# The router logits of a finished item move from between two steps into the next step's first layer

## The chip, the cores and the metric

One core of one Trainium2 chip runs the whole program as one launch. The metric is the device time of that launch in microseconds, as the median of several runs. Before the change it is 465.76 us.

## What is computed

Attention over blocks (8 heads, 576 positions, 2 batches) gives 1152 rows of 512 numbers. Two mixtures of experts follow, each with 8 experts of two layers (512 to 1024 to 512), and each row goes to one expert:

```python
x = _moe_ref(x=x, **moe_kwargs)
return _moe2_ref(x=x, **moe2_kwargs)
...
logits = x @ w_gate
e_idx = np.argmax(logits, axis=1)
...
h = np.maximum(x[mask] @ w1[e], 0.0)
ye = h @ w2[e]
out[mask] = gate_w[mask, None] * eom[mask, e, None] * ye
```

The second mixture needs `logits = x @ w_gate` of the first one's output, for all rows, before it can pick the expert of each row. It also keeps the rows in their order, since an expert takes no more than a given number of them.

## The kernel before

The rows of one mixture are grouped by expert into **items** of up to 128 rows. In this data the first mixture has 10 items (0 to 9), which the program learns at run time. One **step** handles one item: `layer1` (L1254, products at L602), a relu on ScalarE (L1261), 8 transposes on TensorE (`htrans`, L1267), and `layer2` (L1286, products at L616). The inputs are 32-bit floats, and each matrix is split in two parts: `split` (L167) rounds a chunk of weights on ScalarE into `wh` (L147) and puts the rest into `wl` on VectorE (L165); `hsplit` (L1277) does the same with the hidden rows (`hh`, `hl`), and `xprep` (L586) with the item's input (`xh`, `xl`). Each product is then three products (`wh` by `xh`, `wl` by `xh`, `wh` by `xl`), so each layer of a step is 24 products of 512 columns. `raw` holds the weights that DMAs of the SP queue bring (L175 for the first layer's four chunks, L177 for the second's); a DMA waits until the split of the chunk that stood there is done.

Steps overlap by hand. `layers(s)` (L786) runs the first layer of item s, the splits of its second layer's weights, and the second layer of item s-1. `go_on(s)` (L808) splits the first layer's weights of item s+1 and transposes the hidden rows of item s. `finish(s)` (L822) ends the mixture: it loads the first expert of the second mixture, runs the last second layer, and splits what has arrived. Behind the attention part the scheduler is off (L1225), so each engine's queue holds its instructions in the order in which this code issues them, and a wait holds up all that stands behind it on that engine.

The **router logits** of the second mixture are summed item by item in `lg2`, in three parts. `next_a` (L1299) transposes an item's output `ys` (L1302) and copies it to `yt` (L1308). `next_b` (L1312) multiplies it by the router's weights (four products of 8 columns, L1316) and has VectorE spread the result over the row blocks in `nr` (L1318). `next_c` (L1321) multiplies `nr` by a 0/1 matrix that puts each row in its place (one product of 81 columns, L1325), and VectorE adds that to `lg2` (L1327). In steps 2 to 8 `go_on` issues them: `next_b` between the third and the fourth split, `next_c` behind the transposes of the hidden rows. The second mixture's own route for its first item (`side`, L1331, with products at L266, L290, L316 and L318) is woven into steps 6 to 9 by `tick` (L751). When the last item's logits are in, the second mixture chooses its experts and starts (L195 and after).

## Time and profile before

| what | value |
|---|---|
| median of 3 runs (lowest to highest) | 465.76 us (465.01 to 465.87) |
| the profiled execution: its time, and its span from first to last instruction | 467.06 us, 464.9 us |
| busy in the span: TensorE, VectorE, ScalarE, GpSimd | 91%, 80%, 71%, 19% |
| mean granted TensorE clock | 0.959 of full speed |

The rows of the trace name engines as PE (TensorE products), PEld (its weight loads), DVE (VectorE), ACT (ScalarE), POOL (GpSimd) and SP (the queue that issues DMAs). A row of the timeline has the start in us from the span's beginning, the time it took, engine, line, operation, output<-input, size and count; in brackets stands how long the engine had been idle before it, and what ended that. Instructions of one engine overlap by a little: a row's start less the start of the row before is what the engine was held. Attention takes the first 125 us or so, the first mixture runs from there to about 310 us, and the second one to the end.

### The profile page before, as it was taken

What the parts mean: (1) busy time and instruction counts of PE and PEld (TensorE: products, weight loads), DVE (VectorE), ACT (ScalarE), POOL (GpSimd) and SP (SyncE); (2) the same over time, 40 slices, a digit from 0 to 9 for tenths busy, and PEclk for the clock granted to TensorE, in tenths of its full rate; (3) what the DMA queues carried; (4) which work ended last, traced back from release to release, by engine and by line L of the source; (5) the groups of instructions that cost most, each with busy time, mean ns of one, the idle gap of its engine ahead of it and who ended that gap; (6) DMA issues with size and microseconds to landing.
All of it is one profiled execution on the core that took longest, in us unless ns stands there. A gap on an engine that the chain in (4) does not pass through costs nothing. (4 is left out here: it accounts for less than half of the span.)

```text
span 464.9 us, 8359 instructions
## 1 busy us (share of the span) xinstructions
PE 423.7 (91%) x2501; PEld 341.1 (73%) x2501; DVE 369.8 (80%) x816; ACT 328.8 (71%) x617; POOL 87.9 (19%) x182
## 2 busy tenths in 40 slices
PE   4899999999979996999979899688898999999993
PEld 3678887877757765888858688566676888888872
DVE  8666776667898999698878796668889999999940
ACT  3678787787785886587783665635769888898840
POOL 9401222021021203011130301112203111111100
PEclk9999999999988997999997899799998999999998
DMA  5567434011291201199319102901836516996100
GB/s 135 102 198 224 108 77 114 17 27 52 76 357 29 91 0 47 46 314 364 126 46 328 69 1 80 357 25 54 291 127 241 207 45 234 380 379 237 34 29 8
DMA packets 58243, 65.97 MB, mean 142 GB/s; under 512 B 34080, under 2 KB 38688, under 8 KB 58180
## 3 DMA queue, kind: packets, MB, share of 16 engines
q1 hardware_dynamic: 54660, 54.62, 36.2%
q0 software_dynamic: 3520, 10.63, 6.5%
q8 instruction: 25, 0.41, 0.4%
q14 instruction: 38, 0.31, 0.2%
HBM read 109.66 MB, written 11.01 MB: 260 GB/s over the span
## 5 line engine op out<-in xcount | busy, mean ns | idle before, releaser
L165 DVE TENSOR_TENSOR wl<-raw,wh 128x1024 fp32r<-128x1024 f32 x84 | 99.1, 1222 | 9.7 <-ACT wh L147 9.6
L147 ACT CAST wh<-raw 128x1024 fp32r<-128x1024 f32 x84 | 82.7, 1054 | 6.3 <-DMA raw<-in_moe_w_dram 6.2
L602 PE MATMUL ph<-wh,xh 128*128 128x512 f32 x168 | 72.6, 432 | 2.8 <-ACT xh L591 2.1
L602 PE MATMUL ph<-wl,xh 128*128 128x512 f32 x168 | 70.3, 418 | 1.4 <-DVE wl L165 1.4
L602 PE MATMUL ph<-wh,xl 128*128 128x512 f32 x168 | 70.4, 419 | 0.2
L165 DVE TENSOR_TENSOR wl_a<-raw,wh_a 128x1024 fp32r<-128x1024 f32 x44 | 51.6, 1217 | 1.6 <-ACT wh_a L147 1.1
L1037 DVE TENSOR_REDUCE mx<-s 128x1 f32<-128x256 f32 (+8 forms) x72 | 34.4, 487 | 17.4 <-ACT ot L1094 6.1
L147 ACT CAST wh_a<-raw 128x1024 fp32r<-128x1024 f32 x44 | 43.6, 1058 | 5.2 <-DMA raw<-in_moe_w_dram 5.2
L165 DVE TENSOR_TENSOR wl_b<-raw,wh_b 128x1024 fp32r<-128x1024 f32 x40 | 46.9, 1217 | 0.4
L1040 ACT ACTIVATE p<-s,mx 128x256 f32<-128x256 f32 (+8 forms) x72 | 37.9, 528 | 9.7 <-DVE mx L1037 8.7
L602 PEld LDWEIGHTS ph<-wh,xh 128*128 128x128 f32 x168 | 34.5, 205 | 10.4 <-ACT xh L591 2.8
L602 PEld LDWEIGHTS ph<-wl,xh 128*128 128x128 f32 x168 | 34.4, 205 | 10.3 <-DVE wl L165 3.5
L602 PEld LDWEIGHTS ph<-wh,xl 128*128 128x128 f32 x168 | 33.9, 202 | 9.0 <-DVE xl L592 1.7
L1264 ACT ACTIVATE hs<-ph 128x512 f32<-128x512 f32 x38 | 22.2, 599 | 24.1 <-PE ph L602 22.7
L147 ACT CAST wh_b<-raw 128x1024 fp32r<-128x1024 f32 x40 | 39.3, 1062 | 0.0
L1063 PE MATMUL pst<-ident,p 128*128 128x128 f32 x200 | 38.4, 284 | 0.4 <-DVE lg L1109 0.3
L616 PE MATMUL py<-wh_a,hh 128*128 128x512 f32 x88 | 35.3, 401 | 0.4 <-ACT hh L1281 0.4
L616 PE MATMUL py<-wh_a,hl 128*128 128x512 f32 x88 | 34.5, 392 | 0.9 <-DVE hl L700 0.6
L616 PE MATMUL py<-wl_a,hh 128*128 128x512 f32 x88 | 34.4, 391 | 0.0
L616 PE MATMUL py<-wh_b,hh 128*128 128x512 f32 x80 | 32.8, 410 | 0.0
L1089 PE MATMUL pst<-tp,vn 128*64 128x128 f32 (+2 forms) x384 | 31.9, 289 | 0.1
L616 PE MATMUL py<-wh_b,hl 128*128 128x512 f32 x80 | 31.8, 397 | 0.0
(298 smaller groups left out, 866.8 us busy)
## 6 DMA issues: line engine op xcount, KB each, us to landing
raw<-in_moe_w_dram SPq DMA_DIRECT2D x184, 512.0 KB
out_dram<-zrow SPq DMA_DIRECT2D x9, 256.0 KB
kn<-in_k_dram SPq DMA_DIRECT2D x16, 128.0 KB
qn<-in_q_dram SPq DMA_DIRECT2D x16, 128.0 KB
vn<-in_v_dram SPq DMA_DIRECT2D x16, 128.0 KB
x1d<-x SPq DMA_DIRECT2D x3, 576.0 KB
x2d<-zrow SPq DMA_DIRECT2D x3, 256.0 KB
x1d<-x SPq DMA_DIRECT2D x3, 192.0 KB
```

The costliest lines, as they stand in the source:

```text
L147: nc.scalar.copy(whs[i], raw[:, c, :])
L165: V.tensor_tensor(wls[i], raw[:, c, :], whs[i].bitcast(F32), op=ALU.subtract)
L602: yield nc.tensor.matmul(out_, l[:, c * P : (c + 1) * P], r[:, cols], start=(c == 0 and j == 0), stop=(c == KD - 1 and j == 2))
L616: nc.tensor.matmul(y, l[:, cs], r[:, rs], start=(first and j == 0), stop=(last and j == 2))
L1037: V.tensor_reduce(out=s["mx"][:, t : t + 1], in_=ps[:, o : o + n], op=ALU.max, axis=AX.X, negate=True)
L1040: nc.scalar.activation(s["p"][b][:, 0:n], ps[:, o : o + n], AF.Exp, bias=s["mx"][:, t : t + 1], accum_out=s["sm"][:, t : t + 1])
L1063: last[0] = nc.tensor.transpose(ps[:, j * P : (j + 1) * P], s["p"][b][:, c * P : (c + 1) * P], ident).ins
L1089: nc.tensor.matmul(po[r, 0 : n * BLK], nat["v"][h % NR["v"]][:, c, r], w[:, :, r], start=(c == 0), stop=(c == nc_ - 1))
L1264: nc.scalar.activation(hs[:, i * 512 : (i + 1) * 512], hp[i], AF.Relu)
```

## The change

In the first mixture `go_on` no longer issues `next_b` and `next_c`; the next call of `layers` does, inside its first layer. `layer1` takes up to three calls to make behind its chunks 0, 1 and 2: `next_b`'s products, then the first split of the second layer's weights and `nr`, then `next_c`'s product. Its addition to `lg2` is issued behind the third split. In `finish` the transposes of the hidden rows, `next_b`, the scaling of the last but one output and `hsplit` come ahead of the first split of the next expert's weights, and one chunk instead of two is split ahead of `next_a`. The second mixture has no `next_b` and `next_c`.

```diff
--- before.py
+++ after.py
@@ -629,7 +629,7 @@
         def __init__(self, m, R, w1, w2, table, dest):
             self.m, self.R, self.w1, self.w2, self.table, self.dest = m, R, w1, w2, table, dest
             self.st = {n: {} for n in ("w1", "w2", "xg", "xs", "ht", "ys")}
-            self.ahead = self.side = None
+            self.ahead = self.side = self.ga = None
             self.at = {}
         def gather(self, s):
@@ -788,8 +788,24 @@
             R, st, m = self.R, self.st, self.m
             ht = hsplit(st["ht"].pop(s - 1))
-            hp = layer1(st["xs"].pop(s), st["w1"].pop(s))
-            st["w2"][s] = [split(KD + c, s % 2) for c in range(KF // 2)]
+            w2 = st["w2"][s] = []
+            xs, ws = st["xs"].pop(s), st["w1"].pop(s)
+            if self.ga is None:
+                hp = layer1(xs, ws)
+            else:
+                late = []
+                first = lambda: late.append(next_b(R, s - 3, self.ga, True))
+                def second():
+                    w2.append(split(KD, s % 2))
+                    late.append(late.pop()())
+                hp = layer1(xs, ws, (first, second, lambda: late.append(next_c(late.pop(), True))))
+            while len(w2) < KF // 2:
+                w2.append(split(KD + len(w2), s % 2))
+                if self.ga is not None and len(w2) == 3:
+                    late.pop()()
             if s + 1 < NI:
                 self.load(s + 1)
             self.hs = relu(hp)
@@ -810,12 +826,8 @@
             R, st, m = self.R, self.st, self.m
             if s + 2 < NI:
                 self.gather(s + 2)
-            ws = st["w1"][s + 1] = [split(c) for c in range(KD - 1)]
-            gb = next_b(R, s - 2, self.ga) if m == 1 else None
-            ws.append(split(KD - 1))
+            st["w1"][s + 1] = [split(c) for c in range(KD)]
             st["ht"][s] = htrans(self.hs)
-            if gb:
-                next_c(gb)
             self.tick()
             self.store(s - 1, self.y)
@@ -834,17 +846,17 @@
             er = tiles_of(2, "b_")([1], "er", I32)
             nc.scalar.copy(er, first2["er"])
-            self.ws0 = [split(c) for c in range(2)]
+            ps = htrans(self.hs)
+            gb = next_b(R, s - 2, self.ga)
+            self.store(s - 1, self.y)
+            ht = hsplit(ps)
             load_w(*self.ahead[:2], nc.sync.value_load(er[0:1, 0:1], min_val=0, max_val=E - 1), KD, 8)
-            self.store(s - 1, self.y)
-            gb = next_b(R, s - 2, self.ga)
-            ps = htrans(self.hs)
+            self.ws0 = [split(0)]
             next_c(gb)
-            ht = hsplit(ps)
             ga = next_a(R, s - 1, st["ys"][s - 1])
             XH.i = XL.i = 0
             self.xs0 = xprep(xg, PX.next())
-            self.ws0 += [split(c) for c in range(2, KD)]
+            self.ws0 += [split(c) for c in range(1, KD)]
             y = self.y = PY.next()
             for f in range(KF):
                 l2_mm(y, ht, st["w2"][s], f)
@@ -1251,11 +1263,14 @@
     PR = ring(ps_m, [P, 512], F32, "pr", 1)
     rings = [XG, XH, XL, HS, HH, HL, YS, YT, NQ, NR_, PH, PX, PY]
-    def layer1(xs, ws):
+    def layer1(xs, ws, after=()):
         out_ = [PH.next() for _ in range(2)]
         for c in range(KD):
             for i in range(2):
                 l1_mm(out_[i], xs, ws[c], c, slice(i * 512, (i + 1) * 512))
+            if c < len(after):
+                after[c]()
         return out_
     def relu(hp):
@@ -1309,22 +1324,27 @@
         nq, nr = ready or next_places(R, s)
         return yt, nq, nr
-    def next_b(R, s, g):
+    def next_b(R, s, g, late=False):
         yt, nq, nr = g
         pl = PX.next()
         for c in range(KD):
             nc.tensor.matmul(pl[:, 0:E], yt[:, c * P : (c + 1) * P], wg2s[:, c, :], start=(c == 0), stop=(c == KD - 1))
         sh = [P, NT, E]
-        V.tensor_tensor(nr[:, :, 0:E], pl[:, 0:E].unsqueeze(1).to_broadcast(sh), R.of("oht", s).unsqueeze(2).to_broadcast(sh), op=ALU.mult)
-        return nq, nr
-    def next_c(g):
+        def put():
+            V.tensor_tensor(nr[:, :, 0:E], pl[:, 0:E].unsqueeze(1).to_broadcast(sh), R.of("oht", s).unsqueeze(2).to_broadcast(sh), op=ALU.mult)
+            return nq, nr
+        return put if late else put()
+    def next_c(g, late=False):
         nq, nr = g
         pn = PX.next()
         nc.tensor.matmul(pn[:, 0 : NT * (E + 1)], nq, nr.rearrange("p t e -> p (t e)"), start=True, stop=True)
         fl = lg2.rearrange("p t e -> p (t e)")
-        V.tensor_tensor(fl, fl, pn[:, 0 : NT * (E + 1)], op=ALU.add)
+        add = lambda: V.tensor_tensor(fl, fl, pn[:, 0 : NT * (E + 1)], op=ALU.add)
+        return add if late else add()
     route1.pst = route2.pst = PX.next
     one = Moe(1, route1, w11, w12, x1d, x2d[:, :])
```

How the queues change. First TensorE between step 2 and step 3: behind item 1's second layer come the transposes of item 2's hidden rows (`hs`) and item 3's first layer (`ph`). Before:

```order
L1316 MATMUL px_2148<-wg2s,yt_2140 128x8 x4
L1273 MATMUL px_2149<-ident,hs_2135 128x128 x4
L1273 MATMUL px_2150<-ident,hs_2135 128x128 x4
L1325 MATMUL px_2151<-nr_2144,nq_2142 128x81
L602 MATMUL ph_2146<-wh_140,xh_154 128x512
L602 MATMUL ph_2146<-wl_144,xh_154 128x512
```

Now:

```order
L1288 MATMUL px_2148<-ident,hs_2135 128x128 x4
L1288 MATMUL px_2149<-ident,hs_2135 128x128 x4
L602 MATMUL ph_2146<-wh_140,xh_154 128x512
L602 MATMUL ph_2146<-wl_144,xh_154 128x512
...
L602 MATMUL ph_2147<-wh_140,xl_156 128x512
L1331 MATMUL px_2150<-wg2s,yt_2140 128x8 x4
L602 MATMUL ph_2146<-wh_141,xh_154 128x512
...
L602 MATMUL ph_2147<-wh_142,xl_156 128x512
L1344 MATMUL px_2151<-nr_2144,nq_2142 128x81
L602 MATMUL ph_2146<-wh_143,xh_154 128x512
```

The first layer no longer stands behind the product that reads `nr`: 18 of its 24 products come ahead of it, six behind. Next VectorE in the same place, with the four splits of the first layer's weights (`wl`), the two of the hidden rows (`hl`) and those of the second layer's (`wl_b`). Before:

```order
L592 TENSOR_TENSOR xl_156<-px_2151,xh_154 128x512
L165 TENSOR_TENSOR wl_144<-raw,wh_140 128x1024
L165 TENSOR_TENSOR wl_145<-raw,wh_141 128x1024
L165 TENSOR_TENSOR wl_146<-raw,wh_142 128x1024
L1318 TENSOR_TENSOR nr_2144<-px_2148,a_oht_2052 128x9x8
L165 TENSOR_TENSOR wl_147<-raw,wh_143 128x1024
L1327 TENSOR_TENSOR lg_137<-lg_137,px_2151 128x81
L1282 TENSOR_TENSOR hl_2138<-px_2149,hh_2136 128x512
L1282 TENSOR_TENSOR hl_2139<-px_2150,hh_2137 128x512
L165 TENSOR_TENSOR wl_b_2123<-raw,wh_b_2119 128x1024
```

Now:

```order
L592 TENSOR_TENSOR xl_156<-px_2151,xh_154 128x512
L165 TENSOR_TENSOR wl_144<-raw,wh_140 128x1024
L165 TENSOR_TENSOR wl_145<-raw,wh_141 128x1024
L165 TENSOR_TENSOR wl_146<-raw,wh_142 128x1024
L165 TENSOR_TENSOR wl_147<-raw,wh_143 128x1024
L1297 TENSOR_TENSOR hl_2138<-px_2148,hh_2136 128x512
L1297 TENSOR_TENSOR hl_2139<-px_2149,hh_2137 128x512
L165 TENSOR_TENSOR wl_b_2123<-raw,wh_b_2119 128x1024
L1335 TENSOR_TENSOR nr_2144<-px_2150,a_oht_2052 128x9x8
L165 TENSOR_TENSOR wl_b_2124<-raw,wh_b_2120 128x1024
L165 TENSOR_TENSOR wl_b_2125<-raw,wh_b_2121 128x1024
L1346 TENSOR_TENSOR lg_137<-lg_137,px_2151 128x81
```

`nr` stood behind three splits and now stands behind four, both `hl`, and the first split of the second layer's weights. Last VectorE in `finish`, in the branch that this data takes, where `wl` are the splits of the second mixture's first weights. Before:

```order
L165 TENSOR_TENSOR wl_144<-raw,wh_140 128x1024
L165 TENSOR_TENSOR wl_145<-raw,wh_141 128x1024
L1318 TENSOR_TENSOR nr_2145<-px_2150,oht_2570 128x9x8
L1327 TENSOR_TENSOR lg_137<-lg_137,px_2149 128x81
L1282 TENSOR_TENSOR hl_2138<-px_2151,hh_2136 128x512
L1282 TENSOR_TENSOR hl_2139<-px_2148,hh_2137 128x512
L1308 COPY yt_2140<-px_2150 128x512
L1295 TENSOR_SCALAR nq_2142<-i_80,pi_2572 128x128
L592 TENSOR_TENSOR xl_155<-px_2151,xh_153 128x512
L165 TENSOR_TENSOR wl_146<-raw,wh_142 128x1024
L165 TENSOR_TENSOR wl_147<-raw,wh_143 128x1024
L1318 TENSOR_TENSOR nr_2144<-px_2148,oht_2570 128x9x8
```

Now:

```order
L1335 TENSOR_TENSOR nr_2145<-px_2148,oht_2570 128x9x8
L1297 TENSOR_TENSOR hl_2138<-px_2150,hh_2136 128x512
L1297 TENSOR_TENSOR hl_2139<-px_2151,hh_2137 128x512
L165 TENSOR_TENSOR wl_144<-raw,wh_140 128x1024
L1346 TENSOR_TENSOR lg_137<-lg_137,px_2149 128x81
L1323 COPY yt_2140<-px_2150 128x512
L1310 TENSOR_SCALAR nq_2142<-i_80,pi_2572 128x128
L592 TENSOR_TENSOR xl_155<-px_2151,xh_153 128x512
L165 TENSOR_TENSOR wl_145<-raw,wh_141 128x1024
L165 TENSOR_TENSOR wl_146<-raw,wh_142 128x1024
L165 TENSOR_TENSOR wl_147<-raw,wh_143 128x1024
L1335 TENSOR_TENSOR nr_2144<-px_2148,oht_2570 128x9x8
```

The first `nr` and both `hl`, which the last second layer needs, no longer stand behind splits of weights that are still on their way; the second `nr` now stands behind three splits instead of two. The queues of SP and of POOL hold the same instructions in the same order as before.

## Rows read from the trace of the kernel before

**Rows 1.** The page, busy time by engine: TensorE.
```profile
PE 423.7 (91%) x2501; PEld 341.1 (73%) x2501; DVE 369.8 (80%) x816; ACT 328.8 (71%) x617; POOL 87.9 (19%) x182
```
**Rows 2.** Busy time by stretches of 10 us; columns in the first line.
```profile
core 0: us, PE busy (x) PEld busy (x) DVE busy (x) ACT busy (x) POOL busy (x), PEclk, DMA share, GB/s
...
200.00:210.00 10.00, 10.00 (x50) 8.36 (x49) 9.94 (x12) 8.91 (x11) 0.55 (x1) 1.00 0.93 327
...
240.00:250.00 10.00, 6.64 (x25) 5.25 (x23) 9.90 (x23) 4.84 (x6) 2.99 (x3) 0.66 0.74 255
```
**Rows 3.** What TensorE waited for from 145 to 315 us: total, times, longest.
```profile
PE px L1325 <- DVE nr L1318: 11.6, 4, 3.7
```
**Rows 4.** Timeline between step 2 and step 3, VectorE and TensorE.
```profile
178.24 3.48 DVE L165 TENSOR_TENSOR wl<-raw,wh 128x1024 fp32r<-128x1024 f32 x3
...
181.64 0.22 DVE L1318 TENSOR_TENSOR nr<-px,a_oht 128x72 f32<-128x72 f32 x1
...
182.01 0.68 PE L1325 MATMUL px<-nr,nq 128*128 128x81 f32 x2 [2.44 <-DVE nr L1318]
...
184.27 4.62 DVE L165 TENSOR_TENSOR wl_b<-raw,wh_b 128x1024 fp32r<-128x1024 f32 x4
...
190.60 0.60 PE L1302 MATMUL px<-ident,ys 128*128 128x128 f32 x4
```
**Rows 5.** Timeline of steps that TensorE paces (steps 4 and 9).
```profile
211.72 0.23 DVE L1318 TENSOR_TENSOR nr<-px,oht 128x72 f32<-128x72 f32 x1 [1.20 <-PE px L1316]
...
276.65 0.95 PE L1316 MATMUL px<-wg2s,yt 128*128 128x8 f32 x8
...
278.37 0.35 PE L1325 MATMUL px<-nr,nq 128*128 128x81 f32 x2
278.51 0.48 PE L602 MATMUL ph<-wh,xh 128*128 128x512 f32 x1
278.82 0.39 PE L602 MATMUL ph<-wl,xh 128*128 128x512 f32 x1
...
284.07 0.60 PE L1302 MATMUL px<-ident,ys 128*128 128x128 f32 x4
```
**Rows 6.** Timeline between step 6 and step 7.
```profile
239.92 3.49 DVE L165 TENSOR_TENSOR wl<-raw,wh 128x1024 fp32r<-128x1024 f32 x3
...
246.93 1.22 DVE L165 TENSOR_TENSOR wl_b<-raw,wh_b 128x1024 fp32r<-128x1024 f32 x1
...
252.30 0.60 PE L1302 MATMUL px<-ident,ys 128*128 128x128 f32 x4
```
**Rows 7.** Timeline between step 7 and step 8.
```profile
259.19 3.48 DVE L165 TENSOR_TENSOR wl<-raw,wh 128x1024 fp32r<-128x1024 f32 x3
...
265.65 1.22 DVE L165 TENSOR_TENSOR wl_a<-raw,wh_a 128x1024 fp32r<-128x1024 f32 x1
...
270.32 0.60 PE L1302 MATMUL px<-ident,ys 128*128 128x128 f32 x4
```
**Rows 8.** Timeline from step 9's second-layer splits to the last logits.
```profile
280.34 4.61 DVE L165 TENSOR_TENSOR wl_b<-raw,wh_b 128x1024 fp32r<-128x1024 f32 x4
...
288.14 2.49 SPq L175 DMA_DIRECT2D raw<-in_moe_w_dram  x4
...
292.08 1.04 ACT L147 CAST wh<-raw 128x1024 fp32r<-128x1024 f32 x1 [4.23 <-DMA raw<-in_moe_w_dram]
...
298.03 0.68 DVE L1308 COPY yt<-px 128x512 f32<-128x512 f32 x1
...
298.34 0.78 PE L616 MATMUL py<-wh_b,hh 128*128 128x512 f32 x1
...
302.56 0.23 DVE L1318 TENSOR_TENSOR nr<-px,oht 128x72 f32<-128x72 f32 x1
...
306.12 0.39 PE L602 MATMUL ph<-wh,xh 128*128 128x512 f32 x1
...
310.39 0.24 DVE L1327 TENSOR_TENSOR lg<-lg,px 128x81 f32<-128x81 f32 x1 [0.60 <-PE px L1325]
```

## The prediction

> **What bounds the kernel now.** I read the page first: TensorE is busy for 91% of the span [rows 1], so the question is where the other 9% lies. The table of stretches, taken through the first mixture, shows two kinds of step. From 200 to 210 us TensorE is busy without a gap at a granted clock of 1.00: such steps are TensorE's, and a change of order gains nothing in them. From 240 to 250 us it is busy for 6.64 of 10 us at a clock of 0.66, while VectorE is busy for 9.90 [rows 2]: here VectorE sets the pace. The list of waits names the place: TensorE waits four times, 11.6 us in all and 3.7 us at most, at the logits' product L1325 for `nr` of L1318 [rows 3]. The timeline shows why. Between steps 2 and 3 VectorE does three splits from 178.24 on, and `nr` only at 181.64; L1325 has waited 2.44 us by then, and the whole first layer stands behind it [rows 4].
>
> Each wait costs twice. From L1325 to the end of the first layer (the transposes at L1302) 8.59 us pass in this step (182.01 to 190.60), but 5.70 us in step 9 (278.37 to 284.07) [rows 4, 5]. The 2.9 us between them are the granted clock: it fell to its half level, 1.2 GHz, in the idle time ahead, and the stretch from 240 to 250 us, which holds such a place, shows 0.66 [rows 2].
>
> **The change, part by part.** Nothing is added or removed; every instruction of the logits is there as before. What moves is where first layer, `nr` and L1325 stand, so I walk through the four waits. Some terms first, all from rows. One split holds VectorE for 1.13 us (three from 178.24 to 181.64). L1325 starts 0.37 us after `nr` (181.64, 182.01) [rows 4], and itself holds TensorE for 0.14 (278.37 to 278.51). 24 products take 5.56 us at full clock (278.51 to 284.07); the first of them, behind a narrow product, takes 0.31 (278.51 to 278.82), the others 0.23; so six take 1.45, twelve 2.83 [rows 5]. `nr` and the addition to `lg2` hold VectorE for some 0.15 us each, an estimate from their rows of 0.22 and 0.24 less the overlap [rows 4, 8].
>
> *Step 2 to 3.* From the first split of the first layer's weights to the first of the second layer's, VectorE takes 6.03 us (178.24 to 184.27) [rows 4]. `nr` and the addition leave this stretch: 5.73, so 183.97. Behind that split comes `nr`, at 185.10, and L1325 at 185.47. TensorE can start its first layer when the first split is done, near 179.4; 18 products and the logits' four (0.8 us) take until 184.5, so `nr` comes last, and **a wait of some 1 us stands inside the layer**. Then L1325 and six products: L1302 at 187.06, not 190.60. Gain 3.5 us.
>
> *Steps 4 to 6.* TensorE sets the pace, and the narrow products now cut the layer twice instead of standing ahead of it. I count a slow first product (0.08 more) for each cut, 0.16 a step: 0.5 us lost, gain 3.1. The bounds are nothing and 1 us. Does `nr` come in time here? VectorE stood idle for 1.20 us ahead of `nr` in the old order (at 211.72) [rows 5]; the fourth split now fills that time. `nr` needs two `hl` and one split more, and I get it near 214.9, L1325's turn near 216.5: 1.6 us to spare.
>
> *Step 6 to 7.* VectorE's splits start behind a product of the route that follows the second layer, so they move with TensorE: from 239.92 to 236.86. To the second layer's first split it takes 7.01 less 0.30 (239.92 to 246.93) [rows 6]: 243.57. `nr` 244.70, L1325 245.07, L1302 246.66, not 252.30. Gain 5.6.
>
> *Step 7 to 8.* Again behind a route product: splits from 253.55 (L1302 plus 6.89, as from 252.30 to 259.19), second layer's first split 6.46 less 0.30 later, 259.71; `nr` 260.84, L1325 261.21, L1302 262.80, not 270.32 [rows 6, 7]. Gain 7.5.
>
> *Step 9.* TensorE's step of 13.75 us (270.32 to 284.07) plus 0.16 [rows 5, 7]: L1302 at 276.71. VectorE just keeps up: from 265.65 to 280.34 it took 14.69 us, one idle microsecond in it, so its next second-layer split starts near 273.5 and `nr` is there near 274.7, for a turn at 275.1 [rows 7, 8]. Gain 7.4.
>
> *Finish.* The four splits that start at 280.34 end by 284.95; the load of the next expert is issued 3.19 us later (288.14), and its first chunk is read at 292.08 [rows 8]. The old order had `nr` and `hl` wait for two of these chunks. Now VectorE's last split ends near 278.4, the load goes out at 281.6 and arrives at 285.5. TensorE ends step 9's second layer at 283.04 (L1302 plus 6.33, as from 270.32 to 276.65) [rows 5, 7]; transposes and logits take 1.72 (276.65 to 278.37), two `hl` (an estimate of 0.6 each) and the transposes behind them lead to 286.9 for the last second layer, not 298.34. **What is late next** is the second `nr`, behind three splits: yt to `nr` took 4.53 us (298.03 to 302.56) with two splits; with three and a `yt` near 287.9 it is 293.6 [rows 8]. L1325, the wait ended, starts at 293.9, and twelve products end at 296.9. Before, the layer ended at 306.12 [rows 8]. Gain 9.2.
>
> From there to the last addition at 310.39 [rows 8], and in all that follows, order and work are unchanged, and the second mixture's loads wait for what this addition decides. So the shift stays. In the finish several hand-overs are counted at nothing; I take 0.4 us off. **Gain 8.8**: the profiled execution's 467.06 us would be 458.26. It stands 1.30 us above the median of the runs, 465.76, so I give **457.0**.
>
> **Rivals.** *The clock falls at the new gaps.* The forecast has TensorE at full clock in all four places, where it still has gaps of 1 to 2.5 us. A fall costs at most 2.9 us a layer; where TensorE waits for `nr` anyway the wait hides part: 1.1 us between steps 2 and 3, and likewise 2.0 and 1.4 at the next two. Left are 1.8, 0.9 and 1.5 us, and up to 2.4 in the finish: 6.6 in all, 463.6 us; with half of it 460.3. For it: the finish, whose stretch from 283.0 to 286.9 holds transposes and narrow products alone. Against: in TensorE's steps 1.86 us of these stand between the layers (276.65 to 278.51) [rows 5], and the clock stays at 1.00 [rows 2]; the idle time was what the slow places had beside them. The Trainium skill, page "TensorE: Matmul & The Clock Gate", section on the PE-mode transpose, says that transposes don't count as activity for the clock as other products do. By that rule the finish falls, and the time is 2.4 us more, 459.4; the sum doesn't take it, since no row here shows a fall without idle time. 17%.
>
> *The load doesn't move.* If something else than the last split sends out the load at 288.14, such as the branch ahead of `finish`, the first chunk is still read at 292.08. Then `yt` comes near 294.5, `nr` at 300.2, the layer ends near 303.5: gain 2.6, 463.2 us. For it: 3.19 us lie between split and issue, unexplained by these rows. Against: SP's queue has the loads of step 9 ahead, and they wait for these very splits. 6%.
>
> *Every step waits, slower.* If `nr` comes 1.6 us later than I have it in steps 4 to 6, L1325 stops TensorE inside the layer in each step. A stop with a fall of the clock costs 2.9 us in each of steps 4, 5, 6 and 9, which have no such cost today: 11.6 us; with the falls of the first rival (6.6) that is 18.2 against 8.8: 9.4 us slower, 475.2. It decides at 1.6 us, and the idle 1.20 us in VectorE speak against it [rows 5]. 3%.
>
> *Nothing comes through*: another limit past 310 us takes up the gain, 465.8. The page shows none; 3%.
>
> **How the numbers follow.** The forecast has 71%, with 455.2 to 459.2 for its own hand-overs and restarts. The range reaches up into the first rival and to 462.0, and leaves out most of the load's case and both others: 455.2 to 462.0. A measurement of this kernel tells 0.2%, 0.9 us, from no change. Faster by more than that: 71, 17 and 6%, so 94%, of which I give 1 to mixtures of the cases: 93%; the same 3%, slower 4%.
>
> **What would show it.** Right: the wait of L1325 for `nr` is gone ahead of the layers; waits near 1 to 2.5 us at L1325 inside the layers behind steps 2, 6 and 7, none in steps 4 to 6; first layers of 24 products near 5.6 us plus the cuts; granted clock at 1.00 around 181 to 188, 243 to 249 and in the finish; L1302 near 187, 247, 263; the last second layer at 287; one wait near 2.3 us in it for the second `nr`; the last addition near 301.5. Wrong: a clock of 0.5 to 0.7 there, a first chunk still read at 292, L1325 waiting in every step, or a gain at 310 us that the end of the span does not show.

## The result, and the profile after

The changed kernel takes 454.51 us (median of 5 executions, 453.02 to 461.02), the kernel before 465.01 us beside it (5 executions, 462.81 to 465.87): a ratio of 0.9766, interval 0.9734 to 0.9797. That is 2.5 us below the forecast and 0.7 us below the range. A ratio here leaves out executions more than 1.5% above the quickest of their kernel; of these five that is the one that was profiled first, 461.02 us, 6.5 us above the median.

In all, the unaltered changed kernel was executed 14 times here. Seven times lie from 453.02 to 455.31 us and seven from 458.28 to 461.02, none between; the middle of all 14 is 456.8 us, where no execution lies. The mean granted clock is 0.987 to 0.992 in the seven quicker ones and 0.969 to 0.981 in the seven others. So this is a kernel with two kinds of execution, and the text below shows both: its **first profile** (461.02 us) and its **fifth** (453.06 us). The lines have moved: L1302 is now L1317, L1308 L1323, L1316 L1331, L1318 L1335, L1325 L1344, L1327 L1346.

The page's line of busy time, which answers to [rows 1], first profile and then fifth:

```profile
PE 421.2 (92%) x2501; PEld 338.2 (74%) x2501; DVE 369.0 (80%) x816; ACT 328.5 (72%) x617; POOL 93.0 (20%) x182
```

```profile
PE 412.7 (92%) x2501; PEld 331.4 (74%) x2501; DVE 368.7 (82%) x816; ACT 328.4 (73%) x617; POOL 93.2 (21%) x182
```

The instructions are as many as before. TensorE is busy for 8.5 us longer in the first than in the fifth with the same 2501 products, VectorE and ScalarE for as long: the first thing to see is that TensorE's products themselves took longer.

The waits of TensorE from 145 to 315 us, which answer to [rows 3], first profile:

```profile
PE px L1344 <- DVE nr L1335: 4.9, 3, 3.1
PE ph L602 <- DVE wl L165: 2.9, 4, 1.9
PE px L1344 <- DVE a_gate L220: 1.9, 1, 1.9
```

The 11.6 us ahead of the layers are gone. The longest that are left stand inside them: one wait for `wl`, 1.9 us, in step 3, one at L1344 in step 7 (1.9, booked to L220, which runs right behind `nr` on VectorE and ends 0.1 us after it; L1344 starts 0.37 us after `nr`, as in [rows 4]), one in step 8 (1.3), and 3.1 us for the second `nr` of `finish`. Now the two executions in step 3, on TensorE. The first profile:

```profile
176.10 0.48 PE L602 MATMUL ph<-wh,xh 128*128 128x512 f32 x1
178.43 0.69 PE L602 MATMUL ph<-wl,xh 128*128 128x512 f32 x1 [1.85 <-DVE wl L165]
178.92 0.63 PE L602 MATMUL ph<-wh,xl 128*128 128x512 f32 x1
...
186.53 0.34 PE L1344 MATMUL px<-nr,nq 128*128 128x81 f32 x2
...
188.14 0.60 PE L1317 MATMUL px<-ident,ys 128*128 128x128 f32 x4
```

And the fifth:

```profile
166.79 0.64 PE L1317 MATMUL px<-ident,ys 128*128 128x128 f32 x4
...
174.61 0.48 PE L602 MATMUL ph<-wh,xh 128*128 128x512 f32 x1
176.95 0.50 PE L602 MATMUL ph<-wl,xh 128*128 128x512 f32 x1 [1.85 <-DVE wl L165]
177.28 0.40 PE L602 MATMUL ph<-wh,xl 128*128 128x512 f32 x1
...
182.92 0.42 PE L1344 MATMUL px<-nr,nq 128*128 128x81 f32 x2 [0.89 <-DVE nr L1335]
...
184.61 0.60 PE L1317 MATMUL px<-ident,ys 128*128 128x128 f32 x4
```

The order is the same and the idle time ahead of the second product too, 1.85 us. In the one execution the products behind it take 0.63 us, in the other 0.40. The rows by stretches (columns as in [rows 2]) name the reason, first profile, then fifth:

```profile
180.00:185.00 5.00, 5.00 (x17) 4.23 (x17) 5.00 (x7) 0.94 (x1) 0.39 (x1) 0.50 0.17 52
240.00:250.00 10.00, 8.13 (x39) 6.63 (x38) 9.86 (x24) 3.00 (x4) 0.98 (x1) 0.84 0.87 299
```

```profile
180.00:185.00 5.00, 4.11 (x21) 3.12 (x20) 5.00 (x8) 0.73 (x2) 0.00 (x0) 1.00 0.12 34
240.00:250.00 10.00, 8.14 (x41) 6.59 (x40) 8.69 (x27) 5.57 (x7) 0.00 (x0) 1.00 0.93 332
```

The granted clock is at its half level, 1.2 GHz, in the first and at 2.4 GHz in the second. **The same gap is followed by a fall of the clock in one execution and not in another.** The rest of the first mixture in the fifth profile, transposes, logits' products, load and last addition:

```profile
226.27 0.60 PE L1317 MATMUL px<-ident,ys 128*128 128x128 f32 x4
...
242.48 0.42 PE L1344 MATMUL px<-nr,nq 128*128 128x81 f32 x2 [1.85 <-DVE a_gate L220]
244.16 0.60 PE L1317 MATMUL px<-ident,ys 128*128 128x128 f32 x4
...
258.74 0.42 PE L1344 MATMUL px<-nr,nq 128*128 128x81 f32 x2 [1.34 <-DVE nr L1335]
260.43 0.60 PE L1317 MATMUL px<-ident,ys 128*128 128x128 f32 x4
...
274.29 0.60 PE L1317 MATMUL px<-ident,ys 128*128 128x128 f32 x4
...
278.77 2.66 SPq L175 DMA_DIRECT2D raw<-in_moe_w_dram  x4
...
282.88 1.05 ACT L147 CAST wh<-raw 128x1024 fp32r<-128x1024 f32 x1 [0.40 <-issue]
...
284.46 0.48 PE L616 MATMUL py<-wh_b,hh 128*128 128x512 f32 x1
...
290.47 0.23 DVE L1335 TENSOR_TENSOR nr<-px,oht 128x72 f32<-128x72 f32 x1
290.84 0.42 PE L1344 MATMUL px<-nr,nq 128*128 128x81 f32 x2 [2.31 <-DVE nr L1335]
...
293.89 0.39 PE L602 MATMUL ph<-wh,xh 128*128 128x512 f32 x1
...
298.16 0.24 DVE L1346 TENSOR_TENSOR lg<-lg,px 128x81 f32<-128x81 f32 x1 [0.60 <-PE px L1344]
```

Two rows of the kernel before that complete [rows 4 to 8]:

```profile
169.35 0.64 PE L1302 MATMUL px<-ident,ys 128*128 128x128 f32 x4
...
231.94 0.60 PE L1302 MATMUL px<-ident,ys 128*128 128x128 f32 x4
```

From one start of these transposes to the next the time divides into pieces, in us (before: its first profile; forecast: the prediction's walk; the last column is the changed kernel's first profile, with its falls):

| piece | before | forecast | fifth | first |
|---|---|---|---|---|
| step 2's transposes to step 3's | 21.25 | 17.7 | 17.82 | 19.88 |
| steps 4 to 6 | 41.34 | 41.8 | 41.66 | 41.64 |
| step 7 | 20.36 | 17.8 | 17.89 | 18.59 |
| step 8 | 18.02 | 16.1 | 16.27 | 17.18 |
| step 9 | 13.75 | 13.9 | 13.86 | 13.88 |
| step 9's transposes to the last addition | 26.32 | 24.8 | 23.87 | 26.57 |
| last addition to the end of the span | 154.5 | 154.5 | 152.7 | 152.8 |

The fifth gains 11.5 us over the seven pieces, the forecast 8.9, the first 5.0. Between the first and the fifth lie 6.5 us, as much as 461.02 stands above the median. (The fifth's span of 450.9 us is 1.4 shorter than that of the median execution, 452.3: its step 2 transposes come 1.5 to 3.0 us sooner than in the other four profiles, so that much of it arose ahead of the change.)

### The profile page after: what moved, and what is told of

Same layout as the page of the kernel before. It is cut to its first block, busy times and chain, and to the rows that moved or that the text cites. A ratio compares the mean times of both kernels' runs of the same rounds, so it can differ in the third digit from the quotient of the medians.

```text
span 458.8 us, 8354 instructions
## 1 busy us (share of the span) xinstructions
PE 421.2 (92%) x2501; PEld 338.2 (74%) x2501; DVE 369.0 (80%) x816; ACT 328.5 (72%) x617; POOL 93.0 (20%) x182
## 5 line engine op out<-in xcount | busy, mean ns | idle before, releaser
L602 PE MATMUL ph<-wh,xh 128*128 128x512 f32 x168 | 71.3, 425 | 2.8 <-ACT xh L591 2.1
L602 PE MATMUL ph<-wl,xh 128*128 128x512 f32 x168 | 69.0, 411 | 4.1 <-DVE wl L165 4.1
L602 PE MATMUL ph<-wh,xl 128*128 128x512 f32 x168 | 68.8, 409 | 0.2
L602 PEld LDWEIGHTS ph<-wl,xh 128*128 128x128 f32 x168 | 33.0, 196 | 13.1 <-DVE wl L165 7.2
L602 PEld LDWEIGHTS ph<-wh,xh 128*128 128x128 f32 x168 | 32.9, 196 | 9.4 <-ACT xh L591 2.8
L602 PEld LDWEIGHTS ph<-wh,xl 128*128 128x128 f32 x168 | 32.9, 196 | 8.5 <-DVE xl L592 1.7
L616 PE MATMUL py<-wh_a,hl 128*128 128x512 f32 x88 | 34.5, 392 | 0.8 <-DVE hl L700 0.6
L616 PE MATMUL py<-wl_b,hh 128*128 128x512 f32 x80 | 32.0, 400 | 0.0
```

The lines of the kernel that those rows point to most:

```text
L602: yield nc.tensor.matmul(out_, l[:, c * P : (c + 1) * P], r[:, cols], start=(c == 0 and j == 0), stop=(c == KD - 1 and j == 2))
L616: nc.tensor.matmul(y, l[:, cs], r[:, rs], start=(first and j == 0), stop=(last and j == 2))
```

## The experiments

| kernel | median, us (lowest to highest), executions | ratio to before, interval |
|---|---|---|
| changed kernel, second series | 458.31 (454.02 to 461.00), 6 | 0.9841 (0.9805 to 0.9876) |
| steps only | 460.91 (457.05 to 465.13), 8 | 0.9913 (0.9863 to 0.9963) |
| finish only | 462.39 (458.78 to 466.22), 11 | 0.9956 (0.9930 to 0.9982) |
| product last | 455.83 (452.28 to 458.56), 6 | 0.9816 (0.9779 to 0.9852) |
| nr sooner | 455.58 (453.88 to 456.14), 6 | 0.9786 (0.9752 to 0.9820) |
| both | 453.82 (452.04 to 461.19), 6 | 0.9745 (0.9707 to 0.9782) |
| both, finish last | 452.77 (449.92 to 454.80), 6 | 0.9730 (0.9685 to 0.9775) |
| the same, high parts first | 450.52 (447.54 to 453.03), 6 | 0.9686 (0.9639 to 0.9732) |
| added products | 459.17 (456.49 to 461.19), 6 | 0.9886 (0.9850 to 0.9923) |
| nr in place first | 458.48 (456.51 to 461.52), 6 | 0.9865 (0.9821 to 0.9909) |
| in place, new finish | 456.12 (454.22 to 457.45), 6 | 0.9782 (0.9740 to 0.9824) |
| in place, finish last | 454.63 (453.75 to 456.55), 6 | 0.9770 (0.9730 to 0.9810) |

**The changed kernel again**, with no edit.

> The changed kernel unaltered, for a second profile. The first profile of it shows the first mixture at half clock for a few us each at 178, 246, 298 and 304 us, and its last addition to the logits' sum at 306.0 us, later than the 301.5 that the prediction has, though the median of the runs is below the forecast. Theory W, the walk: in an execution near the median these stretches are gone, the last addition stands at 300 to 302 us, and what the time gains beyond the walk's 8.8 us (some 2 us) arises behind the logits or ahead of step 2, at places that the change does not touch. Theory C, the clock: the first mixture itself gains more than the walk had, the last addition stands at 299.5 us or sooner, because TensorE keeps full clock where the walk still counted waits. Both: 454.5 us, within 1.

> The changed kernel, unaltered, for a third profile, in the hope of an execution without a fall in the first mixture. Theory W: transposes behind the first layers at 186 (step 3), 245.6, 261.9 and 275.8 us as with the old finish, the last addition near 299.5 us, the end 152.7 us later. If it falls again: 188.3 us at the first of them, as twice before.

> The changed kernel, unaltered, for a fourth profile. Theory W: an execution without a fall from 140 us to the last addition has a span near 452.1 us, with the transposes behind the first layers at 186.0, 199.9, 213.8, 227.7, 245.6, 261.8 and 275.7 us and the last addition at 299.4. With falls: 458 to 461 us. The end stands 152.7 us behind the last addition, unless the clock falls near 345 us, then 154.4.

> The changed kernel, unaltered, for a fifth profile: as the fourth.

The second, third and fourth profiles (458.34, 459.73, 459.65 us) fall in step 3 as the first did (19.86 to 19.88 us in the table's first piece), and two of them in `finish` too. Only the fifth shows no half clock from 140 us to the last addition. With the start of step 2's transposes as in the others, its last addition would stand at 299.6 to 301.1 us: W had said 300 to 302, C 299.5 or sooner, so the steps are as the walk had them and the finish a little shorter. The time of both theories, 454.5 us within 1, was missed: the second series has 458.31, since four of its six executions are of the slower kind. The gap of 1.85 us ahead of step 3's second product stands in ten profiles in all, with the versions below; seven of them fall there, and three (the fifth, steps only, and both with finish last) don't.

W's other half, a gain behind the logits, is the table's last row. It came in four of the five profiles: 152.7 to 152.8 us. The third has 154.5 us from its last addition (303.06 us) to the end, and half clock there at another place:

```profile
312.00:316.00 4.00, 3.45 (x9) 2.48 (x8) 3.75 (x6) 3.84 (x5) 2.34 (x2) 0.57 0.23 66
```

**The kernel before again**, with no edit, for that last row.

> The kernel before, unaltered, for a second profile. The first shows half clock at 352 us in the second mixture, which costs 1.7 us in the first item's second layer, while seven of the eight profiles with the new order in any part show full clock there, and the one with the new finish alone shows half. If this execution shows full clock there, the 1.7 us were the state of one execution and nothing that the change does. If it shows half again, the old order brings it about.

> The kernel before, unaltered, for a third profile. If each execution draws the fall near 350 us, one of this and the next profile should show full clock there, and 1.7 us less behind the last addition (152.7 instead of 154.4 us to the end). If the old order brings it about, both show half clock and 154.4 us.

> The kernel before, unaltered, for a fourth profile: as the third.

All three show half clock again, at 349 to 350 us, and 154.4 to 154.6 us to the end. First the kernel before, second profile, then the changed one, third profile, at the same place of the second mixture:

```profile
348.87 0.50 PE L602 MATMUL ph<-wl,xh 128*128 128x512 f32 x1 [0.76 <-DVE wl L165]
...
349.81 0.63 PE L602 MATMUL ph<-wl,xh 128*128 128x512 f32 x1
```

```profile
345.14 0.50 PE L602 MATMUL ph<-wl,xh 128*128 128x512 f32 x1 [0.77 <-DVE wl L165]
...
345.94 0.40 PE L602 MATMUL ph<-wl,xh 128*128 128x512 f32 x1
```

The gaps are alike, the order there is the same, and yet the kernel before falls in 4 profiles of 4 and the changed one in none of 5. That each execution draws it, whatever the order, is hardly so. Of the versions below, finish only, which has the old steps, falls at that place too (half clock from 349.9 us on): that makes five profiles of five with the old order in the steps. But so do high parts first and in place with finish last, two of the other fifteen, so the old order isn't what it takes. In all seven the fall begins within 1.1 us of the second gap's end, and the gaps are as long in the thirteen that keep the clock. What is shown is that the changed kernel didn't fall near 350 us in its five profiles, at a place that it doesn't edit, and that four of them gain 1.8 us by it; why is open.

**The parts of the change.** Steps only: `finish` as before. Finish only: the steps as before. The edit in `finish`, which the one undoes and the other makes alone:

```diff
-            self.ws0 = [split(c) for c in range(2)]
-            load_w(*self.ahead[:2], nc.sync.value_load(er[0:1, 0:1], min_val=0, max_val=E - 1), KD, 8)
-            self.store(s - 1, self.y)
-            gb = next_b(R, s - 2, self.ga)
             ps = htrans(self.hs)
-            next_c(gb)
+            gb = next_b(R, s - 2, self.ga)
+            self.store(s - 1, self.y)
             ht = hsplit(ps)
+            load_w(*self.ahead[:2], nc.sync.value_load(er[0:1, 0:1], min_val=0, max_val=E - 1), KD, 8)
+            self.ws0 = [split(0)]
+            next_c(gb)
...
-            self.ws0 += [split(c) for c in range(2, KD)]
+            self.ws0 += [split(c) for c in range(1, KD)]
```

> The steps' new order with the old order in finish. Theory A, the two parts add up as walked: the load for the next expert goes out near 281.6 us instead of 288.1, its first chunk comes near 285.5, the old finish takes its 6.3 us from there to the last second layer and its 7.8 us to the layer's end, so the layer ends near 299.6 instead of 306.1: 6.5 us gained, 458.5 us, or about 457 with the 1.7 us that the change gained beyond the forecast. Rival B, the finish does it: the steps' gain is lost again in the old finish, since its splits wait for the load: 462 us or more. Rival D, finish adds nothing: 454.5 us, as the whole change.

> The old order in the steps with the new order in finish. Theory A: the four waits of 11.6 us in all stay, the load goes out at 288 us as before and its first chunk comes near 292, but the last second layer no longer stands behind it; what is late next is the second nr behind three splits, near 300.2 us, so the layer ends near 303.5 instead of 306.1: 2.6 us gained, 462.4 us. Rival B: finish carries most of the gain, 456 to 458 us. Rival D: finish adds nothing, 464.5 to 465.5 us.

Steps only, profile of 458.33 us:

```profile
275.75 0.60 PE L1317 MATMUL px<-ident,ys 128*128 128x128 f32 x4
...
280.21 2.84 SPq L175 DMA_DIRECT2D raw<-in_moe_w_dram  x4
...
284.55 1.04 ACT L147 CAST wh<-raw 128x1024 fp32r<-128x1024 f32 x1 [4.98 <-DMA raw<-in_moe_w_dram]
...
288.44 0.69 PE L1344 MATMUL px<-nr,nq 128*128 128x81 f32 x2 [4.43 <-DVE nr L1335]
...
299.11 0.39 PE L602 MATMUL ph<-wh,xh 128*128 128x512 f32 x1
```

The load goes out 8 us sooner than in [rows 8] because the steps end sooner, its first chunk is read at 284.55 and the layer ends at 299.11 (285.5 and 299.6 expected): A, in the profile and in the four executions below 459 us. The other four lie above 463. The old finish now has a wait of 4.43 us for `nr`, behind splits whose weights are on their way, and the clock is at its half level behind it. Finish only keeps the waits, 10.7 us, and stands where A put it, 462.39 us (462.4); but the kernel before was quicker in that series, 463.71 us, so its gain is 1.3 us and not A's 2.6. Steps only gains 2.8 us, the whole 5.4: the steps' gain comes through to the end in full only with the new finish. With two kinds of execution in each median, these are rough.

**The wait inside the layer.** Product last moves the addition too:

```diff
-                hp = layer1(xs, ws, (first, second, lambda: late.append(next_c(late.pop(), True))))
+                hp = layer1(xs, ws, (first, second, lambda: None, lambda: late.append(next_c(late.pop(), True))))
...
-                if self.ga is not None and len(w2) == 3:
+                if self.ga is not None and len(w2) == 4:
```

> The changed kernel, with the logits' product behind the first layer's fourth chunk instead of its third, and its addition behind the fourth split. In the changed kernel TensorE waits three times inside the layer for nr, 4.9 us in all, with six products of 1.45 us behind the wait. Theory A, these waits still bound the steps in which VectorE is late: now the six products fill the wait, each such step ends up to 1.45 us sooner and the clock has less of a gap to fall in; 1 to 4 us gained, 450.5 to 453.5 us. Rival E, VectorE sets these steps whatever stands behind the wait: within 0.9 us of the change, 454.5 us. Rival F, the product now stops the transposes behind the layer in the steps that TensorE paces, and the sum is slower: 455.5 us or more.

`nr` sooner:

```diff
                 def second():
-                    w2.append(split(KD, s % 2))
                     late.append(late.pop()())
+                    w2.append(split(KD, s % 2))
```

> The changed kernel with nr ahead of the first split of the second layer's weights instead of behind it, so one split of 1.13 us sooner. Theory A, the waits inside the layer (1.9 us in step 7, 1.3 in step 8, 0.9 in step 3 where the clock does not fall) bound those steps: each shrinks by up to 1.1 us, 2 to 3 us gained on the change: 451.5 to 454 us in executions without a fall of the clock. Rival E, VectorE sets these steps and the wait only shows it: as the change, 454 to 459 us. Rival F, in the steps that TensorE paces VectorE now waits for the four products with one split more behind it: 0.5 us or more slower in each of four steps, 456 us or more.

> The changed kernel with both: nr one split sooner, and the product that reads it behind the first layer's fourth chunk. Theory A: the product alone took the waits of steps 7 and 8 away (1.4 us sooner at the end of each layer in the profile), so nr's place should bring little more there: 0 to 1 us on top of it, 449 to 451 us of span without a fall of the clock, 451 to 453.5 us of time, 454 to 457 with falls. Rival E: no better than the product alone, 455.8 us, because the falls decide.

Both, finish last:

```diff
-                if f == 3:
+                if f == KF - 1:
                     next_c(gb)
```

> The version with nr sooner and the product last, and in finish too the product that reads nr behind the whole second layer instead of behind its first twelve products. There TensorE waited 2.85 us for nr with twelve products of 0.23 us, 2.8 us, behind the wait. Theory A, that wait bounds the end of the first mixture: the products fill it, the transposes of the last output come 2.5 to 2.8 us sooner, 451 us median, 449.5 in executions without a fall. Rival E, VectorE's late nr and the addition behind it set the end: 0 to 0.5 us gained, 453.3 to 453.8 us.

The waits of TensorE at the logits' product, in product last, in `nr` sooner, and in both with finish last (the 1.0 and 2.9 are those of `finish`):

```profile
PE px L1344 <- DVE nr L1335: 1.0, 1, 1.0
PE px L1344 <- DVE a_gate L220: 0.5, 1, 0.5
```

```profile
PE px L1344 <- DVE nr L1335: 3.2, 2, 2.9
```

```profile
PE px L1344 <- DVE nr L1335: 0.8, 2, 0.5
```

Each edit alone takes the waits of steps 7 and 8 away but for 0.5 and 0.3 us in step 7; these steps take 16.48 and 14.84 us in product last and 16.37 and 14.82 in `nr` sooner (17.89 and 16.27 in the fifth profile). So the wait does bound them, and E falls there. The time shows it less clearly: product last, 455.83 us, would fit F, but its steps 4 to 6 are no slower (13.82 us each against 13.89), and its profile has half clock at 181 and at 290 us; `nr` sooner, 455.58, misses A's range and would fit E. Both together, 453.82, and with finish last, 452.77, have lower medians than either alone, but the intervals of their ratios reach into that of `nr` sooner; the last step, 1.0 us where A said 2.5 to 2.8, isn't told from none by the intervals. In its profile the last output's transposes come 2.0 us sooner behind those ahead of them (11.30 us against 13.32), and then the clock falls.

**Filling the gap.** Added products put 26 unneeded products of 512 columns where TensorE idles:

```diff
+    def keep(out, w, n):
+        for _ in range(n):
+            nc.tensor.matmul(out, w[:, 0:P], w[:, 0:512], start=True, stop=True)
...
         out_ = [PH.next() for _ in range(2)]
+        keep(out_[0], ws[0][0], n)
...
         pn = PX.next()
+        keep(pn, w, n)
```

> The changed kernel with products that compute nothing needed, put where TensorE waits: eight ahead of step 3's first layer (written into its first accumulator, which the first real product then starts afresh), six in step 7, four in step 8 and eight in finish ahead of the product that reads nr. At full clock one takes 0.23 us, so they take 1.84, 1.4, 0.9 and 1.84 us of waits measured at 1.85, 1.87, 1.31 and 2.17. Theory C, the clock falls because TensorE idles there, and in which execution it does is what spreads the change's times from 454 to 461 us: no fall at 178, 247 and 298 us any more, the transposes behind step 3's first layer at 186 us instead of 188.3, times within 452.5 to 455.5 us. Rival H, the fall does not hang on these gaps: the times spread as before, and the fills add what does not fit, 0 to 2 us. Rival K, they do not fit at all: 26 products of 0.23 us, up to 6 us slower.

In the profile the fall at 178 us is gone, as C has it:

```profile
175.00:180.00 5.00, 4.96 (x26) 3.93 (x25) 5.00 (x6) 4.46 (x6) 3.76 (x3) 1.00 0.22 73
180.00:185.00 5.00, 4.13 (x21) 3.12 (x21) 5.00 (x8) 0.72 (x2) 0.00 (x0) 1.00 0.12 32
```

Those at 247 and 298 us are gone too, and in all six executions the mean granted clock is 0.984 to 0.988, where the changed kernel's 14 have 0.969 to 0.992. The last addition stands at 297.75 us. But the time is no better: 459.17 us, where C had 452.5 to 455.5, and the ratio, 0.9886, stands above the changed kernel's two. In the profile (456.49 us, the quickest of the six; the others have none) the loss lies at the far end, 156.6 us from the last addition instead of 152.7:

```profile
435.33 0.38 PE L1293 MATMUL px<-ident,hs 128*128 128x128 f32 x2
438.13 0.88 PE L1293 MATMUL px<-ident,hs 128*128 128x128 f32 x6 [2.42 <-issue]
439.29 0.64 PE L616 MATMUL py<-wh_a,hh 128*128 128x512 f32 x1 [0.28 <-ACT hh L1301]
```

Between the second and third of eight transposes TensorE stands still for 2.42 us with nothing to wait for, and then the clock falls (0.64 us a product). The five profiles of the changed kernel have no such stop. The Trainium skill, page "Runtime: NRT & Kernel Launch", section on instruction fetch mechanics, says that an engine streams its instructions in blocks and that a branch out of the loaded ones makes it wait for a fetch. A stop in the midst of like instructions would fit a wait for instructions. One load of instructions (0.02 MB, queue 8) does run in the trace between 435.5 and 438.2 us; but the fifth profile has one in the same stretch and no stop, so no run here shows which it was.

High parts first fills the gap with work that is needed, in step 3 alone:

```diff
         out_ = [PH.next() for _ in range(2)]
+        for low in (0, 1):
+            for c in range(whole):
+                for i in range(2):
+                    l1_part(out_[i], xs, ws[c], c, slice(i * 512, (i + 1) * 512), low)
...
+                if c >= whole:
+                    l1_mm(out_[i], xs, ws[c], c, slice(i * 512, (i + 1) * 512))
```

`l1_part` makes the products of `wh` with `xh` and `xl`, or that of `wl` with `xh`; `whole` is 2 in step 3, and 0 elsewhere.

> The same, and in step 3 the eight products of the first layer's chunks 0 and 1 that don't need the rounded-off rest of the weights come first, the four that do behind them; no instruction is added. They fill the gap of 1.85 us in which TensorE waits for the first split, with work that is needed. Theory C, the fall near 178 us comes from that gap: no half clock there in the profile, the transposes behind step 3's first layer 2 us or more sooner than in the version with both, and 1.5 to 3 us gained on the last one where that still falls; the times' spread shrinks from below upwards. Rival E, VectorE sets the step: without the fall the layer ends where nr or the splits let it, the same as an execution without a fall today, and the median gains 0 to 1 us. Rival L, as with the added products: TensorE's other order shifts where its instructions wait with nothing to wait for, and the end loses 2 us or more.

```profile
174.47 0.48 PE L608 MATMUL ph<-wh,xh 128*128 128x512 f32 x1
175.69 0.50 PE L608 MATMUL ph<-wh,xl 128*128 128x512 f32 x1 [0.74 <-DVE xl L592]
...
177.41 1.28 PE L608 MATMUL ph<-wl,xh 128*128 128x512 f32 x4
...
182.33 0.60 PE L1328 MATMUL px<-ident,ys 128*128 128x128 f32 x4
```

One wait of 0.74 us is left of 1.85, and no half clock follows. Step 3's transposes come 15.68 us behind step 2's; in the version without it, whose profile doesn't fall there either, 16.65. So the filled gap itself is worth 1.0 us in these two profiles. The median, 450.52 us, is 2.3 us lower, C's size and not E's. Falls that don't come could be the rest, but that isn't shown: the mean granted clock of the six executions is 0.976 to 0.986, with 0.973 to 0.984 in the version without it, and the two intervals overlap. It has the lowest median here, with no instruction more than the changed kernel, and an interval below the changed kernel's two.

**Nr in place first** undoes the weaving, and asks if it is needed; `layers` and `finish` are those of before. The two versions behind it take the changed kernel's `finish`, and that with the product behind the whole second layer. Against the kernel before:

```diff
-            ws = st["w1"][s + 1] = [split(c) for c in range(KD - 1)]
             gb = next_b(R, s - 2, self.ga) if m == 1 else None
-            ws.append(split(KD - 1))
+            st["w1"][s + 1] = [split(c) for c in range(KD)]
             st["ht"][s] = htrans(self.hs)
```

> The kernel before with one move: in go_on the logits' four products and nr are issued ahead of all four splits instead of behind the third; the product that reads nr stays ahead of the first layer, finish is the old one. Theory A, the place inside the layer counts: in the three places where VectorE is late nr now comes some 3.4 us sooner and the waits of 2.4 to 3.7 us go, but in the steps that TensorE paces VectorE waits for the four products with four splits behind it (it waited 1.20 us with one split behind it), so it loses up to 3 us in each of steps 4, 5, 6 and 9: 462 to 469 us. Rival G, it counts only that nr no longer stands behind the splits: as the steps alone, 457 to 461 us.

> The steps with nr ahead of all four splits and the product still ahead of the first layer, with the changed kernel's finish. Behind step 9 the steps alone stood at 273.05 us; the new finish takes 23.8 us from there to the last addition without a fall of the clock, and the end comes 152.7 us later: a span of 449.6, 451.8 us. Theory G, the gain needs only nr's place and the new finish: 451 to 454 us, as good as the change or better. Theory A, the weaving into the layer is what counts: 456 us or more, since the old finish's wait only moved to another place.

> The same, with the product that reads the second nr of finish behind the whole second layer. In the version with nr sooner and the product last this took about 1 us off (453.8 to 452.8). Theory G: 450 to 453 us, beside the 450.5 of the best version so far, which needs three edits more. Theory A: 455 us or more.

A said 462 to 469 us; 458.48 is G's (457 to 461). Steps 4 to 6 take 14.14 us each, only 0.36 more than the 13.78 of before, and VectorE has time to spare there (7.95 of 10 us busy in this stretch, 34.5 of 42 from 186 to 228 us):

```profile
200.00:210.00 10.00, 9.93 (x57) 8.43 (x56) 7.95 (x11) 7.96 (x12) 2.29 (x2) 1.00 0.95 335
```

What it loses, it loses in the old finish:

```profile
287.79 0.69 PE L1324 MATMUL px<-nr,nq 128*128 128x81 f32 x2 [6.51 <-DVE nr L1317]
```

With the new finish it is 456.12 us, just at A's bound, and with finish last 454.63, between the two. Its ratio, 0.9782, lies between the two of the changed kernel, 0.9766 and 0.9841: as good as the change as far as these intervals tell, which is what G had said, though above G's 451 to 454 us. So the weaving into the layer is not the only way to a gain of this size: what both orders share is that `nr` doesn't stand behind three splits with the first layer behind it, and that the last second layer doesn't wait for the load.

## Why the prediction was wrong, and where it was right

*The steps* were right to 0.2 us where the clock holds: 17.82, 17.89, 16.27 and 13.86 us against a walk of 17.7, 17.8, 16.1 and 13.9. The wait that it put inside step 3's layer, some 1 us, is 0.89; in steps 7 and 8 it is 1.85 and 1.34. The loss in steps 4 to 6 is 0.3 us, not 0.5. The wait for the first split, 1.85 us, was in the walk as the time at which TensorE can start, but its risk for the clock wasn't weighed by itself; all four profiled falls in step 3 come behind it.

*The finish* gained a little more than its sum had. In the fifth profile: load 4.5 us behind the transposes (4.9 in the walk), last second layer 10.2 (10.2), second `nr` 16.2 (16.9), layer's end 19.6 (20.2); and the 0.4 us taken off for hand-overs weren't lost. The mis-sized term is the way from `yt` to the second `nr`, 5.2 us (285.25 to 290.47) against 5.7. 0.9 us in all.

*The step that failed* is "in all that follows, order and work are unchanged ... So the shift stays". The sum put the stretch behind the last addition at no gain. It took 154.5 us before and takes 152.7 to 152.8 in four of the changed kernel's five profiles, where the half clock near 350 us of all four profiles of the kernel before is absent (the third loses the 1.8 us again at 312.6 us). These two terms, 0.9 and 1.8, less 0.2 us in the steps, are what the fifth profile gains beyond the walk, 11.5 us against 8.9. Measured side by side the gain is 10.5 us against 8.8, since the kernel before took 465.01 us beside it and not 465.76.

That the median came out below the range is in part the draw: four of the first five executions were of the quicker kind, and of all 14 the range of 455.2 to 462.0 holds the seven slower ones and one more. The middle of the 14, 456.8, next to 457.0, would have been luck too, since the forecast meant executions that keep the clock, and these lie at 453.0 to 455.3.

*The first rival*, falls at the new gaps, got 17% and came in half of the executions. Its full price, 6.6 us, is what the first profile shows (6.4 up to the last addition); its times of 460.3 to 463.6 us were too high by much the same as the forecast, since the seven executions with the lower clock lie from 458.28 to 461.02. The argument against it, that a gap of 1.86 us in TensorE's steps leaves the clock at 1.00, held for those gaps alone: they hold transposes and narrow products, the gap in step 3 holds nothing. And forecast and rival were set against one another as if every execution had to be the one or the other alike. The Trainium skill, page "TensorE: Matmul & The Clock Gate", section on what is actually happening, says that the chip's watch on TensorE's activity runs free of the program, so that the place at which a starting kernel comes to full clock differs from run to run. For falls in the midst of a kernel the five profiles fit this: the gap of 1.85 us is followed by a fall in four and not in the fifth. No run here shows the watch itself.

The rule on transposes that the prediction took from the Trainium skill, page "TensorE: Matmul & The Clock Gate", section on the PE-mode transpose, cost nothing here. The stretch of `finish` to which the prediction applied it, 3.8 us of transposes and narrow products alone (280.63 to 284.46 us in the fifth profile), keeps a clock of 1.00 in all five. The falls in `finish`, in three of the five, come some 10 us later, behind the wait of 2 to 3 us for the second `nr`.

*The load* moved as the forecast had it, and the second rival falls: in steps only, where `finish` is the old one, it still goes out 8 us sooner. *Every step waits* falls too: no wait stands at L1344 in steps 4 to 6. *Nothing comes through* falls.

*Open* is what makes the clock fall near 350 us in the kernel before: the gap alone doesn't. Taking that gap away there wasn't tried.

## What to carry to other kernels

A wait in an in-order queue costs what stands behind it, so look at what could stand there instead: moving the late product behind work that is ready, or filling a gap with ready products of the same layer, made a version of 450.5 us where the changed kernel has 454.5 and 458.3 in its two series. Where TensorE keeps a gap like that of 1.85 us in step 3, look for two kinds of executions and forecast both times, not one with a margin. And unneeded products to hold the clock may cost more than they save, as here, where they kept the clock and the median was 459.2 us.

## What was not expected of the hardware

- Two executions of one order, with the same gap of 1.85 us, differ by 2.06 us in step 3, by the granted clock alone; of ten profiles with this gap seven fall.
- Half clock at a place that the change doesn't touch: 4 profiles of 4 before, 0 of 5 after, with the same gaps of 0.76 us. Three of the other versions fall there too.
- 26 added products in TensorE's queue, and a stop of 2.42 us in a straight run of transposes, 145 us behind the last of them.
